# Decode attention beside an MLP: K/V tiles of two neighbouring heads in 32 KB rows, loaded in quarters from GpSimd's queue

## The chip, the cores and the metric

The kernel runs on one core of one Trainium2 chip. The metric is device time in microseconds (us). Before the change three runs gave 211.19, 211.31 and 211.43 us, so the median is 211.31 us.

## What is computed

Four single-token rows `x` (4 x 576) are normalised to `xn`, which feeds two branches:

```
A: q = xn @ wq                      (32 query heads of 128; 16 K/V heads, two query heads to each)
   s = q . k / sqrt(128) over the last 2048 cached positions; p = softmax(s); o = p . v
   A = o.reshape(4, 4096) @ wo
B = xn + gelu(layernorm(xn) @ w3) @ w4     (576 -> 4608 -> 576; the reference's w1, w2 and its
                                            shifts by one position give zero for a single token)
out = x + A + B
```

Everything is bfloat16 in memory. K and V of the window are 2 x 33.6 MB; wq and wo are 4.7 MB each, w3 and w4 5.3 MB each. Every byte is read once.

## The kernel before, in words

**Loads.** All big loads are issued by SP (SyncE) into one DMA queue, in program order. First comes wq (L120, L121), then K/V tiles. A K/V tile holds one head: 128 partitions of 16 KB, each row being 64 positions of 128 bfloat16, contiguous in memory (`load_kv`, L100); one load of 2 MB fills it. Six such tiles exist (`NKV`, L17). `order` (L558) lists the tiles as K0 K1 K2 V0 K3 V1 K4 ...; `flush_loads` (L568) issues the next one as soon as the program has passed the last reader of a tile. wo comes in four parts (L123), w3 after V2 (L128), w4 in six pieces at the very end (L147), a few rows of w4 in a spare K/V tile (L160).

A DMA is given one of eight semaphores in turn, so the DMA with number n waits, in its issuing engine's queue, until number n-8 has landed.

**Start.** GpSimd, VectorE, ScalarE and TensorE build identities and masks, normalise x (L218), transpose it (L233), put x + xn into the accumulator `acc` (L300 to L302: a GpSimd add `xsum`, then a matmul), normalise and transpose once more for branch B (L303 to L305; GpSimd does the power and the copies to `dup`), and only then, in TensorE's order, compute q (L310). From q the block-sparse operand `qz` is made (L341 to L348).

**A head**, in the loop from L591: VectorE transposes K in 32 x 32 blocks, in two halves (`k_transpose`, L252); TensorE makes the scores of all eight (batch, query head) pairs into one PSUM bank of 128 x 512 (`k_scores`, 16 matmuls, after a mask matmul). VectorE takes the maximum per row (`sm_max`); a matmul and a reduction make it the negated maximum per query (`sm_maxT`, `sm_neg`); another matmul of 512 columns adds it to the scores in PSUM (`sm_sub`, L390); ScalarE takes exp (`sm_exp`); VectorE transposes the result (`sm_turn`); 16 matmuls with V make O (`pv`, L420), two steps behind; O is scaled, transposed, summed and, every four heads, multiplied with wo into `acc`. The loop writes the order of every engine out by hand (`manual_schedule`): an engine does its instructions in exactly the order of the program text. The MLP's first half sits in step 7 (`G_AT`), its second half after the last head, where w4 arrives.

Of the kernel before, what the change touches and what calls it, by code (L numbers as in the profile page):

```python
# [16 lines left out]
NKV = 6  # L17
# [5 lines left out]
def kernel(  # L23
# [27 lines left out]
    PB = P // B  # L51
    NC = W // PB
    NJ = B * rep
    QD = 32
    NQD = P // QD
    NSL = 4
    SC = NC // NSL
# [27 lines left out]
    ps_s = ctx.enter_context(tc.tile_pool(name="ps_s", bufs=2, space=PSUM))  # L85
# [14 lines left out]
    def load_kv(kind, h):  # L100
        win = k_win if kind == "K" else v_win
        t = kvp.tile([P, NC, Dh], BF16, tag="kv", name=f"{kind.lower()}n")
        nc.sync.dma_start(out=t[:].rearrange("p c d -> p (c d)"),
                          in_=win[:, h].rearrange("b (p c) d -> p b (c d)", c=NC))
        kv_tiles[kind, h] = t
# [17 lines left out]
    def load_wo(p):  # L123
        t = wop.tile([P, WOR, D], BF16, tag="wo", name="wo_sb")
        nc.sync.dma_start(out=t[:].rearrange("p i n -> p (i n)"), in_=wo_src[p])
        wo_tiles[p] = t

    def load_w3():  # L128
        t = wp.tile([P, KJ * F + F // 2], BF16, tag="w", name="w3_sb")
        nc.sync.dma_start(out=t[:, 0:KJ * F], in_=B_w3[0:KJ * P, :].rearrange("(p j) f -> p (j f)", j=KJ))  # L130
        nc.sync.dma_start(out=t[:, KJ * F:], in_=B_w3[KJ * P:D, :].rearrange("r (e f) -> (r e) f", e=2))
        w_tiles["w3"] = t
# [14 lines left out]
    def load_w4():  # L147
        t = wp.tile([P, NFM, D], BF16, tag="w", name="w4_sb")
        for lo, hi in zip(W4_PIECES, W4_PIECES[1:]):
            e = lo // NFH  # L150
            n = NFH - e
            src = B_w4[e * (F // 2):e * (F // 2) + P * n, :].rearrange("(p i) n -> p i n", i=n)
            nc.sync.dma_start(out=t[:, lo:hi, :], in_=src[:, lo - e * NFH:hi - e * NFH, :])  # L153
        w_tiles["w4"] = t
# [21 lines left out]
    X_AFTER = {13: ["A", (0, 0, 3)], 14: [(1, 0, 3), "B", "C"], 15: [(2, 0, 3), (3, 0, 1), (3, 1, 3)]}  # L176


# [21 lines left out]
    qz = cleared([P, ZP + Hkv * 4 * P], "qz")  # L200
# [3 lines left out]
    accs = [ps_acc.tile([P, CW], F32, name=f"acc{i}") for i in range(2)]  # L204
    for acc in accs:
        nc.vector.memset(acc[:], 0.0)

    def acc_of(i):
        return accs[i * 2 // NI][i * QD:i * QD + B, :]
# [42 lines left out]
    def k_transpose(h, half):  # L252
        c0 = half * 2 * SC
        src = kv_tiles["K", h][:].bitcast(I32)[:, c0:c0 + 2 * SC, :].rearrange("p c (ib i) -> p ib c i", i=QD)
        kt = ktp.tile([P, 2, 2 * SC, QD], I32, tag="kt")
        nc.vector.transpose(out=kt[:], in_=src)  # L256
        kts[h, half] = kt
# [6 lines left out]
    oh4 = const.tile([P, B], F32)  # L264
    nc.vector.reduce_sum(out=oh4[:], in_=ident_f[:].rearrange("p (k b r) -> p b k r", b=B, r=rep), axis=AX.XY)
    ohk = const.tile([P, B], F32)
    nc.vector.reduce_sum(out=ohk[:], in_=ident_f[:].rearrange("p (q b) -> p b q", b=B), axis=AX.X)
    oh_ps = ps_m.tile([B, 2, P], F32, tag="m", name="oh_ps")
    nc.tensor.transpose(out=oh_ps[:, 0, :], in_=oh4[:], identity=ident_f[:])
    nc.tensor.transpose(out=oh_ps[:, 1, :], in_=ohk[:], identity=ident_f[:])  # L270
    ohT = const.tile([B, P], BF16)
    nc.scalar.activation(out=ohT[:], in_=oh_ps[:, 0, :], func=ACT.Copy)
    negbig = const.tile([B, QD], BF16)
    nc.vector.tensor_scalar(out=negbig[:], in0=oh_ps[:, 1, 0:QD], scalar1=-1.0, scalar2=BIG,
                            op0=ALU.add, op1=ALU.mult)

    NG = P // NJ
    sel_j = const.tile([P, NJ], F32)
    nc.vector.reduce_sum(out=sel_j[:], in_=ident_f[:].rearrange("p (g j) -> p j g", j=NJ), axis=AX.X)
    sel_jb = const.tile([P, NJ], BF16)  # L280
    nc.gpsimd.tensor_copy(out=sel_jb[:], in_=sel_j[:])
    sel_g = const.tile([P, NG], BF16)
    with nc.allow_low_precision("zeros and ones"):
        nc.vector.reduce_sum(out=sel_g[:], in_=ident_f[:].rearrange("p (g j) -> p g j", j=NJ), axis=AX.X)
    jT_ps = ps_m.tile([NJ, P], F32, tag="m", name="jT_ps")
    nc.tensor.transpose(out=jT_ps[:], in_=sel_j[:], identity=ident_f[:])
    j_row = const.tile([NJ, P], BF16)
    nc.scalar.activation(out=j_row[:], in_=jT_ps[:], func=ACT.Copy)
    same_j = const.tile([P, P], F32)
    nc.gpsimd.tensor_copy(out=same_j[:].rearrange("p (g j) -> p g j", j=NJ),  # L290
                          in_=sel_j[:].unsqueeze(1).to_broadcast([P, NG, NJ]))
# [6 lines left out]
    nc.vector.reduce_sum(out=own[:], in_=ident_f[:].rearrange("p (h d) -> p h d", h=WOH), axis=AX.X)  # L298

# [38 lines left out]
    for kb in range(NQD):  # L338
        rows = slice(kb * QD, (kb + 1) * QD)
        dst = qz[rows, ZP:].rearrange("p (x m) -> p x m", m=P)[:, :, kb * QD:kb * QD + NJ].rearrange("p x (b r) -> p x b r", r=rep)  # L340
        src = qs_ps[rows].rearrange("p h i r b -> p (h i) b r")  # L341
# [13 lines left out]
    def k_mask(h):  # L355
        S_ps[h] = ps_s.tile([P, NW], F32, tag="S", name="S")
        nc.tensor.matmul(out=S_ps[h][:].rearrange("p (c k) -> p c k", k=QD), lhsT=ohT[:],  # L357
# [3 lines left out]
    def k_scores(h, s):  # L361
        half, c0 = s // 2, s % 2 * SC
        kt = kts[h, half][:].bitcast(BF16)
        if s % 2:
            kts.pop((h, half))
        for ie in range(4):
            ib, e = divmod(ie, 2)
            z0 = (h * 4 + ie) * P + ZP - s * NJ
            nc.tensor.matmul(out=S_ps[h][:], lhsT=qz[:, z0:z0 + P],  # L369
                             rhs=kt[:, ib, c0:c0 + SC, e:2 * QD:2].rearrange("p c k -> p (c k)"),  # L370
                             start=False, stop=False, skip_group_check=True)

    def sm_max(h):
        mx = small.tile([P, 1], F32, tag="mx")
        nc.vector.reduce_max(out=mx[:], in_=S_ps[h][:], axis=AX.X)  # L375
        dm = small.tile([P, NG], BF16, tag="dm")
        nc.vector.tensor_scalar(out=dm[:], in0=sel_g[:], scalar1=mx[:, 0:1], scalar2=None, op0=ALU.mult)
        st["dm", h] = dm

    def sm_maxT(h):  # L380
        mg = ps_m.tile([NJ, NG], F32, tag="m", name="mg")
        nc.tensor.matmul(out=mg[:], lhsT=sel_jb[:], rhs=st.pop(("dm", h))[:], start=True, stop=True)
        st["mg", h] = mg

    def sm_neg(h):
        nm = small.tile([NJ, 1], BF16, tag="nm")
        nc.vector.reduce_max(out=nm[:], in_=st.pop(("mg", h))[:], axis=AX.X, negate=True)  # L387
        st["nm", h] = nm

    def sm_sub(h):  # L390
        nc.tensor.matmul(out=S_ps[h][:], lhsT=j_row[:], rhs=st.pop(("nm", h))[:, 0:1].to_broadcast([NJ, NW]),  # L391
                         start=False, stop=False, skip_group_check=True)

    def sm_exp(h):
        E[h] = ptp.tile([P, SC, QD], BF16, tag="e", name="E", bufs=1)
        if h % 2 == 0:
            st["rs"] = small.tile([P, 2], F32, tag="rs", name="rs", bufs=3)
        nc.scalar.activation(out=E[h][:].rearrange("p c k -> p (c k)"), in_=S_ps.pop(h)[:], func=ACT.Exp, scale=scale,  # L398
                             accum_out=st["rs"][:, h % 2:h % 2 + 1])

    def sm_turn(h):
        PT[h] = ptp.tile([P, SC, QD], BF16, tag="pt", name="PT")
        nc.vector.transpose(out=PT[h][:], in_=E.pop(h)[:])  # L403

    def sm_den(h):
        if h % 2 == 0:
            return
        dn = ps_m.tile([P, 2], F32, tag="m", name="dn")
        nc.tensor.matmul(out=dn[:], lhsT=same_j[:], rhs=st.pop("rs")[:], start=True, stop=True)
        st["dn"] = dn  # L410

    def sm_rec(h):
        if h % 2 == 0:
            return
        rd = small.tile([P, 2], F32, tag="rd", bufs=4)
        nc.vector.reciprocal(out=rd[:], in_=st.pop("dn")[:])  # L416
        for k in range(2):
            st["rd", h - 1 + k] = rd[:, k:k + 1]

    def pv(h, s):  # L420
        if s == 0:
            O_ps[h] = ps_o.tile([P, NSL, Dh], F32, tag="O", name="O")
        vn = kv_tiles["V", h][:].rearrange("p (s c) d -> p s c d", s=NSL)
        for g in range(NQD):
            c = s * NQD + g
            nc.tensor.matmul(out=O_ps[h][g * QD:(g + 1) * QD], lhsT=PT[h][:, c, :], rhs=vn[:, :, c, :],  # L426
                             start=(s == 0), stop=False, skip_group_check=True)
        if s == NSL - 1:
            PT.pop(h)
# [12 lines left out]
    def o_sum(h):  # L442
        oT = st.pop(("oT", h))
        v = oT[:].rearrange("p s (g x) -> p (s g) x", g=NQD)[:, :, 0:NJ].rearrange("p g (b r) -> p b r g", r=rep)
# [3 lines left out]
        with nc.allow_low_precision("summed in float32"):  # L448
            nc.vector.reduce_sum(out=st["on"][:, k * rep:(k + 1) * rep, :].rearrange("p r b -> p b r"),  # L449
# [108 lines left out]
    order = [("K", 0), ("K", 1), ("K", 2)]  # L558
    for h in range(Hkv):
        order.append(("V", h))  # L560
        if h + 3 < Hkv:
            order.append(("K", h + 3))
        if h == min(X_AFTER):
            order.append(("X", h))
    W3_AFTER = ("V", 2)
    pos = {"n": 0, "free": NKV}

# [150 lines left out]
```

## Time and profile before

| | us |
|---|---|
| median of three runs | 211.31 |
| span of the profiled execution, first to last instruction | 209.5 |
| what lies around it | 1.8 |
| DMA engines' packet time on SP's queue, share of the span | 97.7% |
| TensorE busy | 150.2 |
| VectorE busy | 113.3 |
| ScalarE busy | 34.9 |
| GpSimd busy | 9.0 |

Busy times are unions of instruction spans; a matmul's end is modelled, so TensorE's figure is not its share of peak. 87.31 MB move in 209.5 us, a mean of 417 GB/s.

### The profile page before, as it was taken

How to read it: one execution, taken by the hardware profiler on the slowest of the kernel's cores; microseconds unless marked ns; L12 is line 12 of the kernel's file. 1: busy time of each engine (PE TensorE's matmuls, PEld its weight loads, DVE VectorE, ACT ScalarE, POOL GpSimd, SP SyncE). 2: the span in 40 equal slices, each digit the busy share in tenths (PEclk: the TensorE clock that was granted, in tenths of full speed). 3: DMA queues.
4: the chain of work that ended last, by engine and by line, in shares of the span. 5: the costliest groups of instructions: out<-in, count | busy, mean ns of one | idle time of the engine just before them, and what ended most of it. 6: DMA issues, size and time to landing. Idle time of an engine off the chain costs nothing.

```text
span 209.5 us, 2370 instructions
## 1 busy us (share of the span) xinstructions
PE 150.2 (72%) x972; PEld 57.8 (28%) x972; DVE 113.3 (54%) x156; ACT 34.9 (17%) x72; POOL 9.0 (4%) x32
## 2 busy tenths in 40 slices
PE   0457297698690039759998998589696856999783
PEld 0122132233130003213454332224132312343451
DVE  4511877794910083926607889276849390764110
ACT  7602201112010011110222321102111201023100
POOL 4710000000000000000001200000000000000000
PEclk9999589999797556985999999799879985699699
DMA  7999999999999999999999999999999999999992
GB/s 301 400 422 429 425 429 432 422 438 427 456 422 409 446 419 420 444 444 410 441 422 432 444 405 435 438 444 410 438 429 425 428 445 419 432 438 425 427 407 92
DMA packets 6708, 87.31 MB, mean 417 GB/s; under 512 B 761, under 2 KB 1042, under 8 KB 1706
## 3 DMA queue, kind: packets, MB, share of 16 engines
q1 hardware_dynamic: 6690, 87.17, 97.7%
q8 instruction: 7, 0.11, 0.2%
q10 hardware_dynamic: 8, 0.00, 0.0%
q14 instruction: 3, 0.02, 0.0%
HBM read 87.17 MB, written 0.00 MB: 416 GB/s over the span
## 4 chain that ended last, share of the span: by engine, by line
DMA 76%; PE 18%; DVE 3%; ACT 1%; SPq 1%; issue 1%; DVEq 0%; ACTq 0%
DMA vn<-in_A_v_cache_dram 51%; DMA kn<-in_A_k_cache_dram 12%; DMA w_sb<-in_B_w_dram 7%; DMA wq_sb<-in_A_wq_dram 6%; PE S L369 6%; PE O L426 3%; PE g_ps L499 2%; DVE kt L256 2%; PE q_ps L313 2%; PE oT L439 1%; PE acc L215 1%; PE S L391 1%; DVE qz L345 1%; PE gT_ps L521 1%; SPq L153 1%
## 5 line engine op out<-in xcount | busy, mean ns | idle before, releaser
L369 PE MATMUL S<-kt,qz 128*128 128x512 bf16 x256 | 77.6, 432 | 31.6 <-DVE kt L256 31.6
L256 DVE STREAM_TRANSPOSE kt<-kn 128x2048 int32<-128x2048 int32 x32 | 73.5, 2298 | 25.4 <-DMA kn<-in_A_k_cache_dram 24.0
L369 PEld LDWEIGHTS <-qz 128*128 128x128 bf16 x256 | 23.3, 105 | 64.7 <-issue 47.3
L426 PE MATMUL O<-vn,PT 128*32 128x512 bf16 x256 | 24.3, 424 | 9.7 <-DMA vn<-in_A_v_cache_dram 9.6
L398 ACT ACTIVATE E<-S 128x512 bf16<-128x512 f32 x16 | 9.5, 597 | 73.5 <-PE S L391 73.5
L433 ACT ACTIVATE O_sb<-O,rd 128x512 f32<-128x512 f32 x16 | 11.0, 686 | 63.8 <-DVE rd L416 48.3
L403 DVE STREAM_TRANSPOSE PT<-E 128x512 bf16<-128x512 bf16 x16 | 11.4, 710 | 14.4 <-ACT E L398 14.4
L449 DVE TENSOR_REDUCE on<-oT 128x8 bf16<-128x128 f32 x16 | 4.6, 288 | 22.0 <-PE oT L439 21.9
L426 PEld LDWEIGHTS <-PT 128*32 128x32 bf16 x256 | 5.7, 95 | 33.2 <-issue 22.1
L439 PE MATMUL oT<-ident_w,O_sb 128*128 128x128 f32 x64 | 12.7, 335 | 0.0
L375 DVE TENSOR_REDUCE mx<-S 128x1 f32<-128x512 f32 x16 | 10.5, 657 | 0.9 <-PE S L369 0.9
L439 PEld LDWEIGHTS oT<-ident_w,O_sb 128*128 128x128 f32 x64 | 8.3, 167 | 5.1 <-issue 4.7
L391 PE MATMUL S<-nm,j_row 8*128 8x512 bf16 x16 | 6.8, 428 | 1.8 <-DVE nm L387 1.7
L357 PE MATMUL S<-negbig,ohT 4*128 4x512 bf16 x16 | 6.4, 398 | 0.0
L313 PE MATMUL q_ps<-wq_sb,xnT 128*32 128x512 bf16 x40 | 4.1, 591 | 2.2 <-DMA wq_sb<-in_A_wq_dram 2.2
L215 PE MATMUL acc<-w_sb,gT 128*4 128x288 bf16 x70 | 4.9, 286 | 1.1 <-DMA w_sb<-in_B_w_dram 1.1
L499 PE MATMUL g_ps<-w_sb,ln2T 128*32 128x512 bf16 (+2 forms) x55 | 5.5, 439 | 0.0
L541 POOL TENSOR_TENSOR g_u<-g_x 128x180 f32<-128x180 f32 x1 | 0.5, 486 | 102.5 <-ACT g_x L535 102.5
L215 PE MATMUL acc<-wo_sb,op 128*4 128x288 bf16 x64 | 4.6, 286 | 0.4 <-DVE op L471 0.4
L537 DVE COPY g_x<-gT_ps 128x64 f32<-128x64 f32 x2 | 0.5, 225 | 8.1 <-PE gT_ps L521 8.1
L215 PEld LDWEIGHTS <-gT 128*4 128x4 bf16 (+3 forms) x90 | 3.8, 83 | 3.1 <-issue 1.6
L240 PE MATMUL tp<-ident_bf,first 4*128 4x4 bf16 x8 | 0.6, 172 | 5.3 <-DVE first L227 5.3
(94 smaller groups left out, 79.1 us busy)
## 6 DMA issues: line engine op xcount, KB each, us to landing
kn<-in_A_k_cache_dram SPq DMA_DIRECT2D x16, 2048.0 KB, 25.8
vn<-in_A_v_cache_dram SPq DMA_DIRECT2D x16, 2048.0 KB, 23.0
wo_sb<-in_A_wo_dram SPq DMA_DIRECT2D x4, 1152.0 KB, 38.0
w_sb<-in_B_w_dram SPq DMA_DIRECT2D x1, 4608.0 KB
wq_sb<-in_A_wq_dram SPq DMA_DIRECT2D x1, 4096.0 KB
w_sb<-in_B_w_dram SPq DMA_DIRECT2D x1, 2592.0 KB, 10.9
w_sb<-in_B_w_dram SPq DMA_DIRECT2D x2, 576.0 KB, 34.6
w_sb<-in_B_w_dram SPq DMA_DIRECT2D x1, 864.0 KB
```

Of the source, the lines that this page charges most:

```text
L215: nc.tensor.matmul(out=acc_of(i), lhsT=lhsT, rhs=rhs[:, i * CW:(i + 1) * CW], start=False, stop=False, skip_group_check=True)
L256: nc.vector.transpose(out=kt[:], in_=src)
L313: nc.tensor.matmul(out=q_ps[r][g * QD:(g + 1) * QD, :], lhsT=xnT[:, k, :], rhs=wq_sb[:, col:col + NW], start=(j == 0), stop=False, skip_gr ...
L369: nc.tensor.matmul(out=S_ps[h][:], lhsT=qz[:, z0:z0 + P], rhs=kt[:, ib, c0:c0 + SC, e:2 * QD:2].rearrange("p c k -> p (c k)"), start=False ...
L375: nc.vector.reduce_max(out=mx[:], in_=S_ps[h][:], axis=AX.X)
L391: nc.tensor.matmul(out=S_ps[h][:], lhsT=j_row[:], rhs=st.pop(("nm", h))[:, 0:1].to_broadcast([NJ, NW]), start=False, stop=False, skip_grou ...
L398: nc.scalar.activation(out=E[h][:].rearrange("p c k -> p (c k)"), in_=S_ps.pop(h)[:], func=ACT.Exp, scale=scale, accum_out=st["rs"][:, h % ...
L403: nc.vector.transpose(out=PT[h][:], in_=E.pop(h)[:])
L426: nc.tensor.matmul(out=O_ps[h][g * QD:(g + 1) * QD], lhsT=PT[h][:, c, :], rhs=vn[:, :, c, :], start=(s == 0), stop=False, skip_group_check ...
L433: nc.scalar.activation(out=O_sb[h][:], in_=O_ps.pop(h)[:], func=ACT.Copy, scale=st.pop(("rd", h)))
L439: nc.tensor.transpose(out=oT[:, s, :], in_=o[:, s, :], identity=ident_w[:, s * NJ:s * NJ + P])
L499: nc.tensor.matmul(out=out, lhsT=ln2T[:, k, :], rhs=rhs, start=(j == 0), stop=False, skip_group_check=True)
```

## The change

A K/V tile now holds two neighbouring heads (8 pairs, `NPR`): partitions 0 to 63 are the even head, 64 to 127 the odd one, each row 32 KB (128 positions). There are three tiles of 4 MB in place of six of 2 MB. A tile is filled by four loads of 32 partitions (1 MB), in the order of partitions 0, 64, 32, 96. These loads, and wo, w3 and w4, are issued by GpSimd (POOL); wq and the spare rows of w4 stay on SP. The first tiles are requested by `start_loads()`, which stands after the masks and before `xsum`. `free_one` hands a K tile back after its fourth transpose, a V tile after its last `pv`.

A pair's scores fill two PSUM banks (u = 0, 1), each with both heads' queries. The maximum per query is formed once per pair over both banks, multiplied by the scale and used as the bias of the exponential; the matmul of 512 columns that added it is gone. `pv` now takes 64 partitions of P and V at a time: 64 matmuls per pair where there were 32. The loop runs over pairs. The accumulator is one PSUM bank in place of two, and the scores have three in place of two.

```
-NKV = 6
+NKV = 3
...
-        nc.sync.dma_start(out=t[:].rearrange("p c d -> p (c d)"),
-                          in_=win[:, h].rearrange("b (p c) d -> p b (c d)", c=NC))
+        for w in (0, 2, 1, 3):
+            e, half = divmod(w, 2)
+            src = win[:, 2 * t + e, half * (W // 2):(half + 1) * (W // 2), :]
+            nc.gpsimd.dma_start(out=tl[w * QD:(w + 1) * QD].rearrange("p c d -> p (c d)"),
+                                in_=src.rearrange("b (p c) d -> p b (c d)", c=NC))
...
+    order = [("K", 0), ("K", 1)]
+    for t in range(NPR):
+        order.append(("V", t))
+        if t + 2 < NPR:
+            order.append(("K", t + 2))
+    order.append(("X", 0))
+    pos = {"n": 0, "free": NKV}
+    def flush_loads():
+        while pos["n"] < len(order) and pos["free"] > 0:
+            kind, t = order[pos["n"]]
+            if kind == "X":
+                load_x4()
...
+                load_wo(Hkv // WOQ - 1)
+                load_w4()
+            else:
+                if kind == "V" and t % 2 == 0 and t + 2 < NPR:
+                    load_wo(t // 2)
+                load_kv(kind, t)
+            if (kind, t) == ("V", 1):
+                load_w3()
+            pos["n"] += 1
+            pos["free"] -= 1
...
     nc.vector.reduce_sum(out=own[:], in_=ident_f[:].rearrange("p (h d) -> p h d", h=WOH), axis=AX.X)
+    start_loads()
     xsum = xn_f
     nc.gpsimd.tensor_tensor(out=xsum[:], in0=xn_f[:], in1=x_bf[:], op=ALU.add)
     acc_matmuls([(ident_f[0:B, 0:B], xsum)])
...
-    def sm_sub(h):
-        nc.tensor.matmul(out=S_ps[h][:], lhsT=j_row[:], rhs=st.pop(("nm", h))[:, 0:1].to_broadcast([NJ, NW]),
-                         start=False, stop=False, skip_group_check=True)
+    def sm_back(t):
+        bp = ps_m.tile([P, 1], F32, tag="m", name="bp")
+        nc.tensor.matmul(out=bp[:], lhsT=j_row[:], rhs=st.pop(("nm", t))[:], start=True, stop=True)
+        st["bp", t] = bp
+    def sm_bias(t):
+        bias = small.tile([P, 1], F32, tag="bias")
+        nc.vector.tensor_scalar(out=bias[:], in0=st.pop(("bp", t))[:], scalar1=scale, scalar2=None, op0=ALU.mult)
...
+        nc.scalar.activation(out=E[t, u][:].rearrange("p c k -> p (c k)"), in_=S_ps.pop((t, u))[:], func=ACT.Exp,
+                             scale=scale, bias=st["bias", t][:, 0:1], accum_out=st["rs", t][:, u:u + 1])
...
+        for c in range(lo, hi):
+            g = c % NQD
+            for e in range(2):
+                rows = slice(e * 2 * QD, (e + 1) * 2 * QD)
+                nc.tensor.matmul(out=O_ps[2 * t + e][g * QD:(g + 1) * QD], lhsT=PT[t, u][rows, c, :],
+                                 rhs=vn[rows, u, :, c, :], start=(u == 0 and c < NQD), stop=False, skip_group_check=True)
...
+        k_transpose(t, 3)
+        free_one()
...
+            pv(a, 1, SC // 2, SC)
+            free_one()
```

In the built program GpSimd's order at the start is: identities and masks, eight loads (K of pairs 0 and 1) without a wait, wo's first part (waits for load 1), the four loads of V of pair 0 (each waits for the load eight before it: loads 2, 3, 4 and 5), and then `xsum` and the rest of the second normalisation.

## Prediction

> **What bounds the kernel now.** First the page's slices: is an engine full, or is it the DMA?
>
> ```profile
> PE   0457297698690039759998998589696856999783
> DVE  4511877794910083926607889276849390764110
> POOL 4710000000000000000001200000000000000000
> DMA  7999999999999999999999999999999999999992
> GB/s 301 400 422 429 425 429 432 422 438 427 456 422 409 446 419 420 444 444 410 441 422 432 444 405 435 438 444 410 438 429 425 428 445 419 432 438 425 427 407 92
> q1 hardware_dynamic: 6690, 87.17, 97.7%
> ```
>
> The DMA row is 9 from the second slice to the last but one, the compute rows have holes. SP's queue q1 fills 97.7% of the span. So time = bytes / rate + the time in which the engines have nothing to move. The chain that ended last says the same:
>
> ```profile
> DMA 76%; PE 18%; DVE 3%; ACT 1%; SPq 1%; issue 1%; DVEq 0%; ACTq 0%
> ```
>
> So each edit is judged by what it does to the rate, and whether it lets the DMA run dry. Next the start, in order of time, because the change alters who issues there:
>
> ```profile
> 8.44 0.29 POOL L290 COPY same_j<-sel_j 128x128 f32<-128x128 f32 x1
> 8.69 1.26 POOL L301 TENSOR_TENSOR first<-first 4x576 f32<-4x576 f32 x1
> ...
> 11.06 0.42 POOL L237 COPY dup<-first 4x64 bf16<-4x64 bf16 x2 [0.33 <-DVE first L227]
> ...
> 11.36 0.36 PE L242 MATMUL tp<-ident_bf,dup 4*128 4x4 bf16 x2
> ...
> 13.92 4.10 PE L313 MATMUL q_ps<-wq_sb,xnT 128*32 128x512 bf16 x40 [2.21 <-DMA wq_sb<-in_A_wq_dram]
> ...
> 22.33 4.50 DVE L256 STREAM_TRANSPOSE kt<-kn 128x2048 int32<-128x2048 int32 x2
> ```
>
> GpSimd's add at 8.69 leads to TensorE's transposes, which end at 11.72; q waits for wq at 13.92, and the first K transpose starts at 22.33. The last view is VectorE's timeline of the heads whose data was already there:
>
> ```profile
> 31.33 2.30 DVE L256 STREAM_TRANSPOSE kt<-kn 128x2048 int32<-128x2048 int32 x1
> ...
> 45.79 2.29 DVE L256 STREAM_TRANSPOSE kt<-kn 128x2048 int32<-128x2048 int32 x1
> ```
>
> These are the last transposes of heads 1 and 3. Pair 0 of the new kernel (heads 0 and 1) is thus through its K at 33.63, 11.3 us after 22.33, and the next pair at 48.08, 14.4 us later. A pair's K and V are 8.39 MB, 19.5 us at 430 GB/s: compute is faster than the DMA by 5 us a pair.
>
> **Part 1, rows of 32 KB.** In the trace's packet records a 16 KB packet (K, V) has a median of 611 ns, a 32 KB packet (wq's rows) 1213 ns, a 36 KB one (w3's rows) 1364 ns: 429, 432 and 432 GB/s on 16 engines. K and V are 4096 packets now, 2048 afterwards: 128 per engine, each 2 x 611 - 1213 = 9 ns cheaper, a gain of 1.2 us. Loads of K/V go from 32 to 64; if each ends in 16 semaphore packets of 9 ns (757 such packets now), that costs 32 x 9 ns = 0.3 us per engine. Net **-0.9 us**. What GpSimd's queue makes of a row is not in this trace. Bounds: as wq's rows at 432 GB/s, or cut into 4 KB packets, which wq's remainder shows at 159 ns (412 GB/s): 67.1 MB would take 6.5 us more than at 429. I take the first, since all big rows here are moved whole.
>
> SP's queue already fills the engines at 97.7%. [...]
>
> **Part 2, the start.** GpSimd works strictly in order. After `same_j` (now about 9.1: one more small add of 0.3) it issues loads 1 to 8 (K of pairs 0 and 1), wo, and the four quarters of V; the last of them is load 13 and waits for load 5. Behind it stand `xsum` and the second normalisation, and TensorE's matmuls for these stand ahead of q. So q cannot start before load 5 has landed, though wq is there long before. Step by step:
> - Load 5 needs wq and six 1 MB quarters through the engines (5 and 6 travel side by side): 13.9 + 6.29 MB / 0.431 = 28.5.
> - Issue of load 13: 0.6, as an SP issue takes (0.54 to 0.60): 29.1.
> - `xsum` to the end of the `dup` transposes: 11.72 - 8.69 = 3.0: q starts at 32.1 where it was 13.92.
> - q to the first K transpose, 22.33 - 13.92 = 8.4: 40.5. K starts **18 us late**.
> - Pair 0's K is through after 10.4 to 11.3 (the 11.3 above holds 0.9 of a maximum that now comes later): 51.4.
>
> Until then only three tiles are requested: K, K, V and wo's part, 4.19 x 3 + 1.18 = 13.76 MB. They end at 13.9 + 13.76 / 0.431 = 45.8; no tile is free, so the **DMA runs dry**. The next K tile starts at 51.4 + 1.1 (wq's first packet came 1.1 us after its issue) = 52.5: 6.7 us idle. It has landed at 62.2. Pair 1's K is through 12.2 to 14.4 after pair 0's (14.4 from the row; two transposes can run ahead), say 13: 64.4. V of pair 1 then starts at 65.5: 3.3 us idle. Behind it stand w3 (12.3 us) and a K tile freed by V of pair 0 at about 69, so the queue is full again at 87 and stays so. Sum **+10.0 us**. Bounds: if VectorE alone set the pace (4 x 2.3 = 9.2 for pair 0, 11.2 with the maximum, the turn and the small ones for pair 1) and a first byte took 0.6, pair 1's V would start at 40.5 + 9.2 + 11.2 + 0.6 = 61.5 where an unbroken queue starts it at 45.8 + 9.7 = 55.5: 6.0. With 2 us more for GpSimd's issues, 2 us to each first byte, 11.3 and 14.4 it is 15.6.
>
> In the old kernel SP had asked for all that by 6.4 us, and GpSimd's 2.8 us of work ran beside wq: this cover is what goes.
>
> **Part 3, the middle.** At a steady pace a K tile is through 11 us after landing, and one V tile (9.7) plus a K tile (9.7) are queued behind it; so 8 us of slack, and eight 1 MB loads in flight are 19.5 us of work. `mlp_act` stands in GpSimd's order ahead of a K load that waits for `pv` anyway; its 2.3 us of GpSimd time fit. Gone: 16 matmuls of L391, 6.8 us of TensorE; added: 8 small ones, and 256 more of `pv` at 95 ns (24.3 / 256), 24.3 us or 3 us a pair. Both lie under the DMA (in 70 to 120 us TensorE is busy 38.9 of 50): **0**, with 5 us a pair to spare. Without that cover 3 us a pair less 0.8 would show, 18 us at most; below nothing they cannot go, as TensorE sets no transfer here.
>
> **Part 4, the end.** wo's last part and w4 now follow the last V: 6.3 MB, 14.7 us. After that V TensorE has 64 matmuls (6.1), scale, transposes, sums and wo (5.6: a scale of 0.7, and 4.9 from 196.18 to 201.06 for the same steps now), then w4's 48 early matmuls (3.1) and the last ones (1.8): the DMA and TensorE end together. I add **+0.5** (0 to 1.5).
>
> **Sum.** 209.5 - 0.9 + 10.0 + 0 + 0.5 = 219.1 of span; the median lies 1.8 above the span (211.31 - 209.5): **221 us**. Own range: 211.3 + 6.0 - 1.2 = 216 to 211.3 + 15.6 + 0.3 + 1.5 = 228.7.
>
> **Rivals.**
> - **No dry queue, faster.** If pair 0's K were through by 44.7 (45.8 less 1.1) and pair 1's by 54.4, the tiles would be asked for in time; then only part 1 and the end are left: 211.3 - 0.9 + 0.5 = 210.9, or 210.4 with a quiet end. It decides at a first transpose before 31 us (54.4 less 13 and 10.4 to 11.3). For it: wide slack later. Against: the order of GpSimd and load 5's bytes. 0.07.
> - **GpSimd's queue is slower**: cut rows or late requests throughout, 221 + 6.5 to 221 + 10: 227 to 231. Nothing in this trace speaks for either way. 0.13.
> - **Half the engines.** A quarter's source has 8 as its outermost size (32 before). If both quarters in flight went through the same eight engines, 67.1 MB would go at 215 GB/s: 156 us more, about 375. For it: no load of that shape in this trace; against: the order 0, 64, 32, 96 of the partitions puts neighbours into different halves. 0.05.
>
> [...]
>
> **How the numbers follow.** Main case 0.74, the rivals 0.07, 0.13, 0.05, other 0.01. The likeliest gives 221. The range 216 to 231 is the main case's own with the second rival added; the first and third stay out, 0.12 together. A measurement of this kernel tells 0.2% from no change: faster 0.07, same 0.02, slower 0.91.
>
> **What would show it.** In the profile after: q's first matmul near 32 us, the first K transpose near 40, released by GpSimd's `first` and not by wq; two holes in the DMA row near 46 to 52 and 62 to 65, then 9s at 430 or more; GpSimd waiting for `kn` before the add. Wrong would be: q at 14 to 18, holes in the middle, or a mean rate under 420 outside the holes.

## The result and the profile after

The changed kernel takes 226.82 us (median; a second set of five runs on another chip: 226.83), the kernel before 211.31: ratio 1.068, 95% interval 1.061 to 1.075, in the second set 1.071 (1.068 to 1.074). It is 15.5 us slower. One of the first set's four runs, 229.8 us, ran in a slower state, at a lower granted clock (0.864 against 0.878 to 0.885), and is not counted.

The lines below are from the second set. Its profiled execution took 228.8 us (span 227.1), 2 us above the median of its set; experiment 8 shows that these 2 us lie at the end. The page of the changed kernel:

```profile
POOL 5721150012053100220035330303200332110000
...
DMA  7999989808999999999999999999999999999920
GB/s 278 462 439 393 462 383 472 372 0 283 410 271 388 463 422 401 445 412 454 424 416 442 421 421 423 434 452 416 424 450 410 433 442 410 434 403 439 400 86 1
...
q0 software_dynamic: 6656, 82.31, 86.2%
q1 hardware_dynamic: 354, 4.87, 5.2%
...
DMA 51%; DVE 19%; PE 19%; issue 5%; POOL 4%; ACT 1%; DVEq 0%; POOLq 0%; ACTq 0%
```

The bytes are the same; they now take 86.2 + 5.2 = 91.4% of the span where it was 97.7%. The DMA row has a 0 in slice 9 and holes beside it, and one slice too many at the end in which little moves. The chain has VectorE, GpSimd and "issue" in it, which hardly stood there before. GpSimd's start, in order of time:

```profile
8.41 4.48 POOL L108 DMA_DIRECT2D kn<-in_A_k_cache_dram  x8
18.83 0.57 POOL L130 DMA_DIRECT2D wo_sb<-in_A_wo_dram  x1 [5.94 <-DMA kn<-in_A_k_cache_dram]
...
28.57 0.53 POOL L108 DMA_DIRECT2D vn<-in_A_v_cache_dram  x1 [3.81 <-DMA kn<-in_A_k_cache_dram]
29.11 1.26 POOL L337 TENSOR_TENSOR first<-first 4x576 f32<-4x576 f32 x1
...
50.33 2.21 POOL L108 DMA_DIRECT2D kn<-in_A_k_cache_dram  x4 [18.35 <-DVE kt L289]
62.11 2.13 POOL L108 DMA_DIRECT2D vn<-in_A_v_cache_dram  x4 [9.58 <-DVE kt L289]
```

The add that ran at 8.69 runs at 29.11, behind load 13, which waited for a K quarter. What hangs on it, first TensorE's timeline, then VectorE's:

```profile
30.43 1.12 PE L249 MATMUL acc<-first,ident_w 4*4 4x288 f32 x4 [22.22 <-POOL first L337]
...
32.09 3.89 PE L349 MATMUL q_ps<-wq_sb,xnT 128*32 128x512 bf16 x40
```

```profile
39.55 4.50 DVE L289 STREAM_TRANSPOSE kt<-kn 128x2048 int32<-128x2048 int32 x2
45.52 4.51 DVE L289 STREAM_TRANSPOSE kt<-kn 128x2048 int32<-128x2048 int32 x2 [1.47 <-PE S L405]
```

TensorE waits 22.22 us for GpSimd's `first`, not for wq. q is 18.2 us later than before, the first K transpose 17.2. GpSimd's next K load is issued only when pair 0's four transposes are through. The stretches of the same trace (length; busy time of PE, PEld, DVE, ACT, POOL; granted clock, DMA share, GB/s), and the last of them as it was before the change:

```profile
45.00:52.00 7.00, 6.56 (x28) 2.37 (x26) 6.41 (x5) 0.00 (x0) 1.68 (x4) 0.96 0.15 40
52.00:62.00 10.00, 5.83 (x24) 2.09 (x24) 9.72 (x10) 1.45 (x4) 0.53 (x2) 1.00 0.93 364
62.00:67.00 5.00, 4.49 (x41) 1.49 (x42) 2.70 (x7) 0.00 (x0) 3.24 (x6) 0.66 0.94 269
67.00:72.00 5.00, 4.83 (x48) 1.39 (x47) 4.08 (x4) 1.27 (x2) 1.12 (x2) 1.00 0.86 356
72.00:180.00 108.00, 74.81 (x613) 29.74 (x623) 60.95 (x88) 15.02 (x40) 23.77 (x45) 0.82 1.01 429
```

```profile
72.00:180.00 108.00, 85.93 (x511) 31.74 (x511) 65.62 (x82) 16.25 (x42) 2.32 (x5) 0.85 1.01 431
```

The queue is empty from 45 to 52. Afterwards it doesn't come back at 430: the DMA share is 0.93 and 0.94, but only 364 and 269 GB/s move. In the packet records 24 of the 32 large packets that start from 51 to 55 us, and 24 of the 33 from 63 to 67, take 1.8 to 2.6 us each instead of 1213 ns. At 75 us 26.43 MB have moved where it was 31.18: 4.75 MB, or 11.0 us at 0.43 MB per us. From 75 to 200 us it is 53.56 MB against 53.66, no difference to speak of. The other 4.5 us are left for the end.

### The profile page after: what moved, and what is told of

It is laid out like the page before. It is cut to its first block, busy times and chain, and to the rows that moved or that the text cites. A ratio compares the mean times of both kernels' runs of the same rounds, so it can differ in the third digit from the quotient of the medians.

```text
span 228.0 us, 2914 instructions
## 1 busy us (share of the span) xinstructions
PE 141.7 (62%) x1195; PEld 57.5 (25%) x1211; DVE 113.8 (50%) x171; ACT 32.6 (14%) x72; POOL 50.2 (22%) x109
## 4 chain that ended last, share of the span: by engine, by line
DMA 57%; PE 16%; DVE 16%; issue 4%; POOL 4%; SPq 1%; ACT 1%; DVEq 0%; POOLq 0%; ACTq 0%
DMA kn<-in_A_k_cache_dram 33%; DMA wo_sb<-in_A_wo_dram 12%; DVE kt L289 11%; PE S L405 6%; DMA vn<-in_A_v_cache_dram 6%; DMA x<-in_B_w_dram 5%; PE acc L249 4%; PE q_ps L349 2%; POOL kn L108 2%; PE O L476 1%; PE oT L489 1%; DVE PT L446 1%; DMA first<-in_A_x_dram 1%; DVE mx L411 1%; POOL vn L108 1%
## 5 line engine op out<-in xcount | busy, mean ns | idle before, releaser
L289 DVE STREAM_TRANSPOSE kt<-kn 128x2048 int32<-128x2048 int32 x32 | 73.5, 2301 | 44.5 <-DMA kn<-in_A_k_cache_dram 40.7
L108 POOL DMA_DIRECT2D vn<-in_A_v_cache_dram x32 | 17.0, 540 | 72.9 <-DVE kt L289 46.3
L108 POOL DMA_DIRECT2D kn<-in_A_k_cache_dram x32 | 17.4, 556 | 46.4 <-DVE kt L289 18.7
L476 PE MATMUL O<-vn,PT 64*32 64x512 bf16 x512 | 22.6, 429 | 0.0
L441 ACT ACTIVATE E<-S,bias 128x512 bf16<-128x512 f32 x16 | 10.8, 682 | 57.3 <-DVE bias L434 57.3
L249 PE MATMUL acc<-first,ident_w 4*4 4x288 f32 x4 | 1.1, 660 | 21.9 <-POOL first L337 21.9
L456 PE MATMUL dn<-ro,same_j 128*128 128x4 f32 x16 | 3.0, 258 | 13.3 <-DVE ro L450 13.3
L489 PE MATMUL oT<-ident_w,O_sb 128*128 128x128 f32 x64 | 10.7, 299 | 0.4 <-DVE bias L434 0.3
L476 PEld LDWEIGHTS <-PT 64*32 64x32 bf16 x512 | 4.9, 91 | 10.9 <-issue 10.0
L456 PEld LDWEIGHTS dn<-ro,same_j 128*128 128x128 f32 x16 | 2.7, 203 | 16.6 <-issue 13.5
L158 POOL DMA_DIRECT2D w_sb<-in_B_w_dram x6 | 3.2, 535 | 11.8 <-DMA vn<-in_A_v_cache_dram 11.8
## 6 DMA issues: line engine op xcount, KB each, us to landing
vn<-in_A_v_cache_dram POOLq DMA_DIRECT2D x32, 1024.0 KB, 15.6
```

What stands on the lines that cost most here:

```text
L108: nc.gpsimd.dma_start(out=tl[w * QD:(w + 1) * QD].rearrange("p c d -> p (c d)"), in_=src.rearrange("b (p c) d -> p b (c d)", c=NC))
L249: nc.tensor.matmul(out=acc_of(i), lhsT=lhsT, rhs=rhs[:, i * CW:(i + 1) * CW], start=False, stop=False, skip_group_check=True)
L441: nc.scalar.activation(out=E[t, u][:].rearrange("p c k -> p (c k)"), in_=S_ps.pop((t, u))[:], func=ACT.Exp, scale=scale, bias=st["bias", t ...
L456: nc.tensor.matmul(out=dn[:].rearrange("p e u -> p (e u)"), lhsT=same_j[:], rhs=st.pop("ro")[:].rearrange("p e u -> p (e u)"), start=True, ...
L476: nc.tensor.matmul(out=O_ps[2 * t + e][g * QD:(g + 1) * QD], lhsT=PT[t, u][rows, c, :], rhs=vn[rows, u, :, c, :], start=(u == 0 and c < NQ ...
L489: nc.tensor.transpose(out=oT[:, s, :], in_=o[:, s, :], identity=ident_w[:, s * NJ:s * NJ + P])
```

## Experiments

**Theory A**: the loss is the start, where the first loads' waits stand ahead of `xsum` on GpSimd. **B**: the end adds 4 us because w4 and the tail's order leave too much behind the last transfer. **C**: GpSimd's queue, or the quarter loads, move bytes more slowly. Medians are in us, ratios against the kernel before on the same chip.

**1. Loads after the normalisation.**

```
-    start_loads()
...
     transposed(ln2_bf, ln2T)
+    start_loads()
```

> The changed kernel with start_loads() moved behind the second normalisation and its transposes; nothing else. My theory (GpSimd's order puts the waiting V loads ahead of the add that q needs, and the DMA then runs dry): q's first matmul goes back from 32.2 us to 14 to 16, the first K transpose to 22 to 24, the two holes of the DMA between 45 and 70 us (some 11 us of missing bytes) go, and the time falls by 10 to 12 us, to 215 to 217. Rival (GpSimd's queue or quarter loads are slow in themselves): the start moves forward but holes stay, and the time falls by under 4 us.

217.15, ratio 1.026 (1.024 to 1.028), just above the expected 215 to 217. q stands at 13.9, and the holes at 45 to 72 are gone. The first K transpose comes at 25.6, not at 22 to 24: the queue is thin from 12 to 20 us (352 GB/s), since the first K is asked for too late. 9.7 us of the loss go with the start: A.

**2. The last instructions in another order.** `mlp_extra` goes behind the last `o_sum`, w4's first piece ahead of `o_proj`.

```
-    mlp_extra(XB, XS)
     o_turn(2 * hl)
...
+    mlp_extra(XB, XS)
...
+    mlp_out(*pieces[0])
     o_proj(2 * hl + 1)
```

> The changed kernel with another order of the last instructions alone: the transposes of the last two heads ahead of the matmuls with the spare rows of w4, and the first piece of w4 (36 matmuls) ahead of wo. Theory (after the last byte TensorE still has 6.8 us of matmuls in a row, because its order made it wait for the spare rows at 212.8 us): the time falls by 3 to 5 us, to 222 to 224. Rival (the end is set by the arrival of w4 alone): the time does not move by more than 0.5 us.

225.9, ratio 1.069 (1.067 to 1.070): 0.9 gained, not 3 to 5, and the interval overlaps that of the changed kernel (1.068 to 1.074). The order of the last few matmuls is not what makes the end late; B in this form fell. **3. Both edits:**

> Both edits of the two runs before this one. If the two losses are separate they add up: 14 to 16 us below the changed kernel, 211 to 213 us, level with the kernel before. If the late end is a consequence of the late start (compute that lags behind the DMA to the end), the tail's part shrinks and the sum is less than that of the two alone, 214 or more.

216.6, ratio 1.026 (1.024 to 1.028): only 0.5 off for the tail, with the same interval as experiment 1, as the case has it in which the tail is a consequence.

**4. The old kernel with its big loads on GpSimd** (`nc.sync` to `nc.gpsimd` in `load_kv`, `load_wo`, `load_w3`, `load_w4`; nothing else).

> The kernel before, with its 2 MB loads of K and V and those of wo, w3 and w4 issued by GpSimd in place of SP; rows of 16 KB, one head per tile, its loads still behind the start's work in program order. Theory (the queue itself costs nothing, only what waits behind it): 211 to 213 us. Rival (GpSimd's queue moves the same rows more slowly): 217 us or more.

212.97 (8 runs), ratio 1.007 (1.004 to 1.010). The queue itself costs 1.6 us in the median; two of the eight runs, 211.5 and 211.6, show almost nothing of it. In the profiled run (213.3 us) the bytes fall 0.18 MB behind in 115 to 125 us, where GpSimd's `mlp_act` stands ahead of a load, and the last large packet ends at 207.8 where it was 205.45, with only an engine or two still moving from 206.5 on. C is true, but small, and it does not show in every run.

**5. Eight loads ahead, the rest behind.** Experiment 3 with `start_loads()` back in its place, but with only two tiles to give; the third is given after the normalisation.

```
-    pos = {"n": 0, "free": NKV}
+    pos = {"n": 0, "free": 2}
...
     transposed(ln2_bf, ln2T)
+    free_one()
```

> As e3, but the eight loads of the first two K tiles stand again ahead of the add (they wait for nothing, so they join the queue while wq still moves), and only wo's part and V of pair 0, which wait for landings, stand behind the second normalisation. Theory A (a gap between wq and the first K load costs a slow restart: 0.76 MB behind at 20 us, 1.8 us): the start moves 430 GB/s without a dip as in the changed kernel, q starts at 16 to 17, and the time falls 1.5 to 2 us below e3, to 214.5 to 215.1. Theory B (quarter loads start slowly because of their shape, gap or not): no change from e3, 216.6.

214.5, ratio 1.013 (1.009 to 1.017). GpSimd's timeline of this kernel:

```profile
8.44 4.46 POOL L108 DMA_DIRECT2D kn<-in_A_k_cache_dram  x8
12.87 1.26 POOL L337 TENSOR_TENSOR first<-first 4x576 f32<-4x576 f32 x1
...
18.76 0.62 POOL L130 DMA_DIRECT2D wo_sb<-in_A_wo_dram  x1 [3.07 <-DMA kn<-in_A_k_cache_dram]
```

The same eight issues, but none that waits ahead of the add: 12.87 instead of 29.11. q stands at 15.9, and the stretches between 8 and 200 us (of 4 us and more) all move 414 GB/s or more; at 20 us 7.58 MB have moved, as before (7.57), at 75 us 31.17 (31.18). Against experiment 2, which has the same tail, the start's share is 225.9 - 214.5 = 11.4 us. So the start is closed, and 3.2 us are left.

**6 and 7. Who issues w4.** Experiment 5 with w4 and wo's last part on SP; then in addition the spare rows of w4 on GpSimd, so that none of SP's loads waits for them.

```
-            nc.gpsimd.dma_start(out=t[:, lo:hi, :], in_=src[:, lo - e * NFH:hi - e * NFH, :])
+            nc.sync.dma_start(out=t[:, lo:hi, :], in_=src[:, lo - e * NFH:hi - e * NFH, :])
```

> As e6, with w4 and the last part of wo issued by SP. Theory (at the end GpSimd's queue runs out unevenly: 413 and 326 GB/s in the last stretches of e3, the last packet 4.5 us later than in the kernel before): a further 1 to 2 us off e6, 213 to 214. Rival (the ragged end belongs to the pieces, whoever issues them): within 0.3 us of e6. Second rival: SP's loads overtake the last V and delay it, 2 us or more above e6.

217.2, ratio 1.028 (1.025 to 1.031). The queue is nearly dry at 190 to 194 (117 GB/s), since SP's loads wait 5.2 us for a spare-row load that landed late. This says nothing about the ragged end.

> As the run with the split start, but w4 and the last piece of wo are issued by SP, and the spare rows of w4 by GpSimd, so that none of SP's issues waits for the lane of a spare-row load that lands late. If the ragged end (the last 1 to 2 us, in which only one or two engines still move bytes) belongs to GpSimd's queue, the last large packet ends near 205.5, as before, and the time is 212.5 to 213.0. If the ragged end belongs to the pieces, whoever issues them, the time stays at 214.5. If SP's loads get between GpSimd's last V loads, the last V lands later and the time is 216 or more.

227.67, ratio 1.077 (1.073 to 1.081), 13 us slower than experiment 5. SP, with nothing to wait for, asked for wo's last part and all of w4 early: 6.1 of their 6.3 MB moved from 155 to 191, ahead of the last K and V. It is the run that decides about the end. VectorE at the last K tile, first in experiment 5, then here; then the stretches after it and TensorE's last V matmuls:

```profile
172.51 2.31 DVE L289 STREAM_TRANSPOSE kt<-kn 128x2048 int32<-128x2048 int32 x1 [5.42 <-DMA kn<-in_A_k_cache_dram]
```

```profile
185.38 2.31 DVE L289 STREAM_TRANSPOSE kt<-kn 128x2048 int32<-128x2048 int32 x1 [17.81 <-DMA kn<-in_A_k_cache_dram]
```

```profile
200.00:205.00 5.00, 5.00 (x65) 1.46 (x63) 1.28 (x3) 0.00 (x0) 1.08 (x2) 0.75 0.98 412
205.00:210.00 5.00, 2.83 (x36) 2.02 (x28) 2.55 (x9) 2.72 (x6) 0.98 (x2) 0.94 0.16 58
210.00:218.00 8.00, 7.14 (x119) 3.86 (x121) 1.76 (x6) 1.27 (x2) 0.00 (x0) 0.83 0.01 2
```

```profile
210.14 3.19 PE L477 MATMUL O<-vn,PT 64*32 64x512 bf16 x64
```

All large packets have ended by 207.2, as in experiment 5 (207.6), w4 is long there, and the span still ends at 225.9. No transfer is left to blame. The last V has landed at 206.3 and is first used at 210.14. K comes 12.9 us later than in experiment 5, and the span ends 12.6 us later. From the last K's first transpose to the end of the span it is 40.5 us here, 40.4 in experiment 1, 39.4 in 3, 40.7 in 5, 40.2 in 2: **the end is a chain of compute that hangs on when the last K tile arrives**, and the 14.7 us of transfers of wo and w4 at the end lie beside it. Putting them ahead of K moved K, and the end with it. Before the change the last K tile held one head, and it was 29.8 us from its first transpose to the end, 25.7 us of it with transfers still to come:

```profile
179.73 2.31 DVE L256 STREAM_TRANSPOSE kt<-kn 128x2048 int32<-128x2048 int32 x1 [1.15 <-DMA kn<-in_A_k_cache_dram]
```

**8. The changed kernel once more** (the profile shown above).

> The changed kernel as it is, once more. The time is 224 to 227, the queue empty at 45 to 52 and thin at 62 to 70 us. If the end belongs to the transfers, the span ends 1 to 2 us behind the last large packet, as before the change; if it belongs to the work that follows the last K tiles, it ends 4 to 7 us behind, with the last large packet near 217 to 218.

226.83. The last large packet ends at 218.0, the span 9.1 us later, where 4 to 7 were expected. Some 2 us of it are this execution's own: up to there it runs like experiment 2, whose span is 2.9 us shorter, 0.9 of it by its edit (first transpose of the last K at 184.13 against 184.04, last large packet at 217.98 against 217.94). Its end, on TensorE:

```profile
203.92 0.62 PE L476 MATMUL O<-vn,PT 64*32 64x512 bf16 x16
...
209.39 3.56 PE L476 MATMUL O<-vn,PT 64*32 64x512 bf16 x64
...
217.00 2.08 PE L249 MATMUL acc<-wo_sb,op 128*4 128x288 bf16 x16 [0.97 <-DVE op L521]
218.87 4.81 PE L249 MATMUL acc<-w_sb,gT 128*4 128x288 bf16 x70
```

The last V tile has landed at 203.2, but the first matmul on it runs at 209.39: the last pair's scores stand behind the V matmuls of the pair before (the x16 groups, to 204.5), and the softmax follows. Then all 70 matmuls of w4 come in a row and wait for nothing: the last of their data landed 0.9 us before the first.

**9 and 10. A shorter chain.** In the last pair the scores and the maximum stand ahead of the V matmuls of the pair before, so that the softmax runs beside these; w4's first load of 18 rows is cut into three of 6, and its matmuls stand where the rows arrive. First on the changed kernel, then on experiment 5.

```
+    k_scores(hl, 3, 0)
...
+    k_scores(hl, 3, 1)
+    sm_max(hl, 1)
...
+    pv(a, 0, 0, SC)
+    sm_maxT(hl)
+    sm_neg(hl)
+    pv(a, 1, 0, SC // 2)
...
+    sm_exp(hl, 0)
+    sm_exp(hl, 1)
+    pv(a, 1, SC // 2, SC)
```

> The changed kernel with its end alone rewritten: the last pair's last scores and its softmax stand ahead of the V matmuls of the pair before, w4's first load of 18 rows is three loads of 6, and w4's matmuls are placed where their rows arrive. The loads' order and the start stay. If the end is the chain of compute that begins with the last K tile (40 to 43 us against 34 us of transfers left), the chain gets about 5 us shorter, the last large packet still ends near 218, the span ends 3.5 to 4.5 us behind it, and the time is 223.0 to 224.5. If the end belongs to GpSimd's queue (its last bytes come late and the rest follows them), the time stays within 1 us of the changed kernel's 226.8.

224.91, ratio 1.064 (1.059 to 1.068), 1.9 under the second set's 226.83 (1.068 to 1.074) and 0.4 short of the expected range. The first set's wider interval (1.061 to 1.075) covers it, so what the edit did is read from the trace. TensorE's end:

```profile
204.04 1.43 PE L476 MATMUL O<-vn,PT 64*32 64x512 bf16 x32
...
209.16 0.90 PE L249 MATMUL acc<-w_sb,gT 128*4 128x288 bf16 x12 [2.38 <-DMA w_sb<-in_B_w_dram]
...
217.14 0.78 PE L249 MATMUL acc<-w_sb,gT 128*4 128x288 bf16 x10 [0.85 <-DMA w_sb<-in_B_w_dram]
218.54 1.02 PE L249 MATMUL acc<-w_sb,gT 128*4 128x288 bf16 x12 [0.63 <-DMA w_sb<-in_B_w_dram]
```

The last V's matmuls start at 204.04, and the three groups of w4 now wait for transfers: the chain has dropped under them. The span ends 4.4 us behind the last large packet, as in the kernel before (4.1).

> The same new end on the kernel with the split start. By the chain theory the span ends 3.5 to 4.1 us behind the last large packet at 207.6, as the kernel before does behind its own, and the time is 212.9 to 213.6. If w4's first rows, which now arrive in three loads, leave holes in the queue, or the end belongs to the queue, it stays at 214.5. Faster than 211.3 only if the last large packet itself came at 205.5, which nothing in this edit brings about.

213.87, ratio 1.011 (1.008 to 1.015): 0.6 less than experiment 5 (1.009 to 1.017), which the overlapping intervals do not tell from nothing, and 0.3 above the expected range. It is the lowest time found, 1.1% above the kernel before; no version here beats that.

**11 and 12. The quarter loads by themselves.** The changed kernel with its K/V quarters issued by SP (`nc.gpsimd` to `nc.sync` in `load_kv`), one run; and with the order of the quarters 0, 32, 64, 96 on GpSimd (`for w in range(4)`), one run.

> The changed kernel with the quarter loads of K and V issued by SP; wo, w3 and w4 stay on GpSimd. If a load with 8 as its outermost size is bound to the same eight engines on SP's queue, K and V go at about half the rate, 215 GB/s, and the time is 340 to 380. If SP spreads them over all 16, the DMA row shows 430 GB/s; GpSimd's add is then not behind V's loads, the early holes go and the time is 213 to 218.

> The changed kernel with the quarters in the order of partitions 0, 32, 64, 96 in place of 0, 64, 32, 96. [...] If where the loads write plays no part, within 2 us of the changed kernel, 224 to 229.

394.2 us, a little above the expected 340 to 380, and 381.5, far above the 224 to 229 expected if where the loads write plays no part. The stretch from 60 to 350 us, columns as above, first the loads on SP, then the other order:

```profile
60.00:350.00 290.00, 117.47 (x809) 42.28 (x821) 93.37 (x126) 20.45 (x52) 6.57 (x13) 0.69 0.55 224
```

```profile
60.00:350.00 290.00, 132.20 (x931) 48.09 (x945) 98.96 (x135) 21.95 (x55) 34.61 (x66) 0.69 1.01 223
```

The rate is the same, the packets are not. On SP the DMA share is 0.55 and a 32 KB packet still takes 1213 ns: about half of the engines work, at full speed. In the other order the share is 1.01 and the median packet takes 2544 ns: all engines work, each at half speed, where the order 0, 64, 32, 96 has 1213 ns and 429 GB/s (72 to 180 us of the changed kernel). So for these loads both the issuer and the order of the quarters halve the rate, each in its own way. Why SP's quarters keep only half of the engines busy, and why the packets of the other order take twice as long, these runs do not show.

## Why the prediction was right, and where it was not

The forecast was 221, the time is 226.8: slower, for the reason given, within the range, but 5.8 us above the number. That it is within the range is partly luck. With part 2 as measured (11.4) and parts 1 and 4 at their upper ends (0.3 and 1.5) the forecast's terms reach 224.5; the rest was covered by room that part 2 had for slow issues and first bytes, and that the end used up. (That room is stated 0.9 us too wide: redone step by step, the upper 15.6 comes to 14.7, since a later first byte of pair 2's K does not delay pair 1's K, from which the second gap is counted.) Nor does the number tell the main case from the rival "GpSimd's queue is slower", which began at 227; the traces do. By its steps:

- **Part 2, the order of GpSimd: right.** Load 13 issued from 28.57 to 29.10 (28.5 to 29.1), q at 32.09 (32.1), first K transpose at 39.55 (40.5), pair 0's K through at 50.03 (51.4), the next K load issued at 50.33 by exactly that release. Experiment 5 moves the one wait and gets 11.4 us back.
- **Part 2, the size: 10.0 forecast, 11.0 to 11.4 measured.** The empty stretch was right (45.8 to 52.5 forecast, 45 to 52 seen). The second, 3.3 us long, shows as a slow one, and that the queue came back at 269 to 364 GB/s was not in the sum. Why the packets after the two requests at 50 and 62 us are slow stays open.
- **Part 1: wrong sign, small.** The 32 KB packet was right (1213 ns). The small packets of a load (four bytes, 9 ns) were put at 16; a quarter load leaves 48 (3264 four-byte packets on GpSimd's queue, of which 192 stay there when experiment 11 moves the 64 quarter loads to SP). Per engine and 4.19 MB it was 16 x 611 + 2 x 9 = 9794 ns and is 8 x 1213 + 12 x 9 = 9812. The gain of 0.9 us doesn't exist: 429 GB/s from 72 to 180 us, and 431 before the change.
- **Part 3: right.** 72 to 180 us run at 429 GB/s; there is no hole. The 256 more V matmuls don't even cost TensorE time (below).
- **Part 4: the failed step.** "The DMA and TensorE end together", +0.5, was counted from the landing of the last V. The path goes from the last K instead: 40 us of compute against 34 us of transfers behind it, with scores queued behind the V matmuls of the pair before. The last V lay there for 6 us. What the end cost is about 4 us: 0.9 for the order (experiment 2), 0.6 more for the chain (10), 1.6 for GpSimd's queue, seen in the old kernel too (4), and 1.0 that is left between experiments 10 and 4. Of these only the 1.6 is clear of noise by itself. Their sum is: with the start closed, experiment 5 is still 1.8 to 3.5 us above the kernel before by its interval.

With the start's 11.4 that is the 15.5 us: 226.8, 225.9 (2), 214.5 (5), 213.9 (10), and 211.3 before. The 1.0 is not traced to one cause; `fin` is a candidate, whose two halves now follow each other (209.92 and 210.40 in experiment 5: ScalarE waits for VectorE's, 0.45 us) and ran side by side before (206.90 and 206.93). It is about as large as the intervals of the two ratios together.

Of the rivals, "half the engines" was the near miss: two details of `load_kv`, the issuer and the order of the quarters, stood between 227 us and 381 or 394. "No dry queue" is experiment 5, and even that is not faster. "GpSimd's queue is slower" holds for 1.6 us in the median.

Not tried: 32 KB rows in a single load of 128 partitions, which needs another layout of the pair; an earlier request for the last K, which needs a fourth tile.

## What to carry to other kernels

When loads move to an engine that also computes, look for the first load that has to wait there, and put no work that the start depends on behind it: here the place of five loads was worth 11 us. Where the DMA is the bound, the end can be set by the chain from a late tile that is not the last one, as here from the last K and not the last V: measure from the arrival of each of the last tiles to the end, and compare it with the transfers still to come. Larger packets brought nothing here, because the loads got smaller at the same time and each left its own small packets (9812 ns per engine and 4.19 MB where it was 9794).

## What was not expected of the hardware

V matmuls of 64 rows cost half as much busy time here as those of 128 rows. The groups, before and after (count; busy us, mean ns of one):

```profile
L426 PE MATMUL O<-vn,PT 128*32 128x512 bf16 x256 | 24.3, 424 | 9.7 <-DMA vn<-in_A_v_cache_dram 9.6
```

```profile
L476 PE MATMUL O<-vn,PT 64*32 64x512 bf16 x512 | 25.3, 477 | 0.0
```

Twice as many take about the same time, 49 ns of busy time each against 95. The mean of one is no shorter, so by these records, in which a matmul's end is modelled, twice as many are under way at a time: 16 in the 0.216 us from 208.480 us in the first set's trace of the changed kernel, 8 in the 0.216 us from 189.700 us before the change, both at a granted clock of 1.00.

The end is now compute, and the same 64 V matmuls of the last pair took 3.56 us in the profile shown (granted clock 0.71 from 210 to 218 us) and 1.92 us in experiment 5 (clock 1.00 from 194 to 200). In the first set the changed kernel's three counted runs lie between 223.7 and 226.8 us, those of the kernel before between 211.2 and 211.4; whether the clock is what spreads them was not tested.
